# One head's K and V loaded in two pieces with different source shapes, in a two-layer decode kernel

## The chip, the cores and the metric

The kernel runs on one core of a Trainium2 chip. Its engines work side by side and meet at semaphores: PE (TensorE: matmuls, and PEld for its weight loads), DVE (VectorE), ACT (ScalarE), POOL (GpSimd) and SP (SyncE, which here only issues transfers). Transfers between the chip's main memory and the on-chip memory of 128 partitions are carried by 16 DMA engines. The metric is device microseconds of one launch, the median of several runs. Most runs of one kernel agree within a few tenths of a per cent. Beside the runs stands one profiled execution, whose trace gives the times of single instructions and packets.

## The reference

Two layers A and two layers B, in the order A, B, A, B, for a single token. A is attention of 32 heads over the last 4096 of 32768 cached keys, and B a mixer with a small MLP. With one token, the shifted part of the mixer is zero (every shifted slice falls off the end), so `w1` and `w2` don't count.

```python
def _A_ref(x, k_cache, v_cache, wq, wo):
    B, Sq, D = x.shape                     # 1, 1, 640
    Hq, Dh = 32, 192
    Hkv, Sk = k_cache.shape[1], k_cache.shape[2]
    W = min(4096, max(256, Sk // 4))       # 4096
    ...
    scores = jnp.einsum("bhqd,bhkd->bhqk", q, k) * (Dh ** -0.5)
    p = _softmax(scores, axis=-1)
    o = jnp.einsum("bhqk,bhkd->bhqd", p, v)
    return (lambda x, *d: x.transpose(*d))(o, 0, 2, 1, 3).reshape(B, Sq, Hq * Dh) @ wo

def _B_ref(x, w1, w2, w3, w4):
    ...
    h2 = _gelu(_layernorm(x1, axis=-1) @ w3) @ w4
    return x1 + h2

x = A_x
x = x + _A_ref(_layernorm(x, axis=-1), A_k_cache, A_v_cache, A_wq, A_wo)
x = x + _B_ref(_layernorm(x, axis=-1), B_w1, B_w2, B_w3, B_w4)
x = x + _A_ref(_layernorm(x, axis=-1), A_k_cache, A_v_cache, A_wq, A_wo)
x = x + _B_ref(_layernorm(x, axis=-1), B_w1, B_w2, B_w3, B_w4)
return x
```

Both layers A read the same K and V: 32 heads x 4096 keys x 192 bf16 values, twice.

## The kernel before

**Data.** The K of one head is 4096 rows of 384 bytes, contiguous in main memory. `Kw(h)` (L67) views it as 128 rows of 6144 values: partition p holds the 32 keys 32p to 32p + 31, 12,288 contiguous bytes. `Vw(h)` (L68) does the same for V. Each is loaded whole into one of 15 slots of that shape, by one DMA on SP's queue (`load`, L98 to L103). The same slots hold the five pieces of `wq` (L92 to L96), the transposed K, and the mixer's weights `w3` and `w4` with a half slot `half` (`load_w34`, L119 to L133). `wo` has its own two buffers (L107 to L112).

**Heads and groups.** The 32 heads form 8 groups of G = 4. Head h = 4g + i. For each head of the next group, `trans` (L254) transposes K on DVE in 32 x 32 blocks, in two halves (L258), and `kmm` (L268) multiplies it with the queries on PE (L280). For the current group `pv` (L337) multiplies the probabilities with V on PE (L349, L355, L360), `evac` scales by the softmax sum on DVE (L372 to L376), and `outproj` multiplies with `wo` (L383). `soft_a`, `soft_b`, `soft_c` (L291 to L333) make the softmax of a group: maximum over all keys of a head, exponentials on ACT (L314), sum over partitions by a matmul with ones (L322), and the probabilities brought into the layout of V. The order of the keys inside K and V matters only in that both have the same one.

**Order.** All of it is a fixed program order, written by hand: `attention` (L390) runs over the groups in `order` and, within a group, over the four heads, doing K work of the next group and V work of this one in turns. `plan` (L493) lists the loads in the order of their use: for each head the K of the next group, then the V of this one; after the second head `wo`; at the end of the layer the mixer's weights. Layer 1 takes the groups 0 to 7, layer 2 takes 7 to 0 and reuses the K (transposed), V and `wo` of what is still there: group 7's K and V are not loaded again, which leaves 60 K and 60 V loads in all.

**Queue.** All loads go through SP's queue in this order. A load waits on SP for its slot to be free (for the transpose or the matmul that read it last), and for the load issued eight before it: the loads use eight semaphores in turn. A load has landed when its semaphore has been increased by 16. Until then SP holds back only what is behind a waiting issue.

**The boundary.** The mixer (L459) reads `w3` (L470) and then `w4` (L487); its slots are free after that, and the K loads of layer 2 go into them. The last weights to come are the two loads of `half` (L129 and L130), which hold the last 20 of the 60 matmuls of L487 (w4's last chunks).

**PE's instructions.** The program is unrolled: 17,337 instructions on PE. They are fetched from main memory during the run, by DMA.

Of the kernel before, what the change touches and what calls it, by code (L numbers as in the profile page):

```python
# [16 lines left out]
P = 128  # L17
G = 4
ACT_TABLE_SET = 6
GELU_C = 0.044715  # L20
GELU_A = -2.0 * (2.0 / 3.141592653589793) ** 0.5
NSLOTS = 15


@with_exitstack
def kernel(
# [14 lines left out]
    nc = tc.nc  # L41
# [14 lines left out]
    NG = H // G  # L56
# [10 lines left out]
    Kw = lambda h: A_k_cache[0, h, s0:Sk, :].rearrange("(p j) d -> p (j d)", p=P)  # L67
    Vw = lambda h: A_v_cache[0, h, s0:Sk, :].rearrange("(p j) d -> p (j d)", p=P)  # L68
# [16 lines left out]

    free = deque(slots.tile([P, FREE], BF16, name=f"slot{n}", tag=f"slot{n}") for n in range(NSLOTS))
    half = slots.tile([P, HALF], BF16, name="half", tag="half")

    def slot():
        return free.popleft()  # L90

    wq_t = []  # L92
    for kc in range(ND):
        t = slot()
# [3 lines left out]
    def load(kind, h):  # L98
        if (kind, h) in resident:
            return  # L100
        t = slot()
        nc.sync.dma_start(t[:], (Kw if kind == "K" else Vw)(h))
        resident[(kind, h)] = t  # L103

    wo_t = {}

# [283 lines left out]
    def attention(order, xT_cur, xT_new, keep, loads):  # L390
        n_loaded = [0]

        def need(upto):
            while n_loaded[0] < min(upto, len(loads)):
                what = loads[n_loaded[0]]
                n_loaded[0] += 1
                if what[0] == "wo":
                    load_wo(what[1])
                elif what[0] == "w34":
                    load_w34()  # L400
                else:
                    load(*what)
# [155 lines left out]
```

## Time and profile before

| | us |
|---|---|
| median of 3 runs | 544.62 |
| lowest, highest | 543.62, 544.75 |
| the profiled execution, its own time | 543.57 |
| its span, first to last instruction | 541.3 |

| engine | busy us | share of the span |
|---|---|---|
| PE | 294.1 | 54% |
| PEld | 273.4 | 51% |
| DVE | 248.8 | 46% |
| ACT | 32.4 | 6% |
| POOL | 2.1 | 0% |

The page says further: 33,871 DMA packets, 219.42 MB, mean 405 GB/s; the granted clock of PE was 1.00 throughout. Times are microseconds from the start of the span. In lines of groups of instructions stand the line of the kernel, the engine, the operation, what it writes and reads, the count, and the mean duration. In the chain of waits each line has the start, the duration, and what ran: it follows the work that ended last back to what released it. SPq is SP's issuing of transfers. Two digit rows show the span in 40 equal slices, each digit the busy share in tenths. The tables by stretch give, for each stretch, its length, the busy time of each engine (with the count of instructions), the clock, the DMA share and the GB/s. A load from L102 took, in the median, 24.1 us (K) and 22.4 us (V) from issue to landing.

### The profile page before, as it was taken

To read this page: it belongs to the slowest core of one execution; us is meant where nothing else is said; L and a number is where in the kernel's file an instruction comes from. 1 tells how busy PE (TensorE), PEld (TensorE's weight loads), DVE (VectorE), ACT (ScalarE), POOL (GpSimd) and SP (SyncE) were. 2 spreads that over 40 slices of the span, in tenths; PEclk is the share of its full clock that TensorE was granted. 3 is DMA by queue.
4 is the path that set the end of the run, shared out by engine and by line. 5 is a ranking of instruction groups with operands and counts; after the bars stand their busy time and mean duration, and the time that the engine had idled before them with its cause. 6 is when DMAs were issued, how large, how long until landed. Compare 5 with 4: busy or idle time off the path is not lost.

```text
span 541.3 us, 18457 instructions
## 1 busy us (share of the span) xinstructions
PE 294.1 (54%) x8730; PEld 273.4 (51%) x8730; DVE 248.8 (46%) x360; ACT 32.4 (6%) x193; POOL 2.1 (0%) x11
## 2 busy tenths in 40 slices
PE   0144555663645536545475666655565655565654
PEld 0043554553645535544464656555555655555554
DVE  1185555354453555443502354565555455545402
ACT  1001010000101001010011100001010101010001
POOL 1000000000000000000000000000000000000000
DMA  8999999999999999999998899999999999999994
GB/s 347 429 426 412 423 422 411 425 411 423 417 418 425 409 424 414 421 422 412 417 410 305 354 420 427 422 413 421 410 423 421 411 421 412 420 420 416 417 401 160
DMA packets 33871, 219.42 MB, mean 405 GB/s; under 512 B 2692, under 2 KB 16516, under 8 KB 17796
## 3 DMA queue, kind: packets, MB, share of 16 engines
q1 hardware_dynamic: 33786, 218.25, 97.9%
q8 instruction: 68, 1.11, 0.8%
q14 instruction: 7, 0.06, 0.0%
q10 hardware_dynamic: 10, 0.00, 0.0%
HBM read 218.24 MB, written 0.00 MB: 403 GB/s over the span
## 4 chain that ended last, share of the span: by engine, by line
DMA 57%; DVE 18%; PE 16%; SPq 3%; issue 2%; ACT 2%; DVEq 0%
DMA slot<-in_A_k_cache_dram 36%; DVE slot L258 16%; DMA slot<-in_A_v_cache_dram 14%; DMA wo_g<-in_A_wo_dram 5%; PE S_ps L280 4%; PE O_ps L349 4%; PE O_ps L360 3%; SPq L129 2%; DMA half<-in_B_w_dram 2%; ACT E L314 2%; PE qT_ps L238 1%; PE l_ps L322 1%; PE nb_ps L308 1%; PE O_ps L355 1%; SPq L128 1%
## 5 line engine op out<-in xcount | busy, mean ns | idle before, releaser
L258 DVE STREAM_TRANSPOSE slot<-slot 128x1536 uint32<-128x1536 uint32 x120 | 206.0, 1756 | 94.7 <-PE O_ps L360 48.1
L280 PE MATMUL S_ps<-Qblk,slot 128*128 128x4 bf16 x3072 | 101.3, 167 | 180.1 <-DVE slot L258 179.6
L280 PEld LDWEIGHTS <-slot 128*128 128x128 bf16 x3072 | 91.3, 104 | 191.4 <-DVE slot L258 190.9
L349 PE MATMUL O_ps<-PT,slot 128*128 128x1 bf16 x2048 | 64.2, 165 | 8.2 <-DMA slot<-in_A_v_cache_dram 7.5
L349 PEld LDWEIGHTS <-slot 128*128 128x128 bf16 x2048 | 61.4, 104 | 13.5 <-DMA slot<-in_A_v_cache_dram 7.9
L360 PE MATMUL O_ps<-PT,slot 128*128 128x1 bf16 x1984 | 63.5, 166 | 2.0 <-issue 2.0
L360 PEld LDWEIGHTS <-slot 128*128 128x128 bf16 x1984 | 58.1, 105 | 3.1 <-issue 2.1
L372 DVE TENSOR_TENSOR osb<-O_ps,rl 128x2 bf16<-128x2 f32 x32 | 5.2, 162 | 72.1 <-PE O_ps L360 72.1
L310 ACT COPY nb_sb<-nb_ps 128x4 f32<-128x4 f32 x16 | 2.6, 162 | 444.3 <-PE nb_ps L308 444.3
L238 PE MATMUL qT_ps<-xn_bf,slot 128*128 128x1 bf16 x480 | 15.9, 165 | 18.3 <-DMA slot<-in_A_wq_dram 17.1
L238 PEld LDWEIGHTS <-slot 128*128 128x128 bf16 x480 | 14.5, 104 | 18.9 <-DMA slot<-in_A_wq_dram 17.5
L242 DVE TENSOR_TENSOR Xq<-qT_ps,maskq 128x24 bf16<-128x24 f32 x16 | 2.9, 182 | 41.1 <-PE qT_ps L238 41.1
L324 DVE RECIPROCAL rl<-l_ps 128x4 f32<-128x4 f32 x16 | 2.9, 179 | 33.2 <-PE l_ps L322 33.2
L314 ACT ACTIVATE E<-S_ps,nb_sb 128x32 bf16<-128x32 f32 x64 | 17.5, 286 | 0.5
L383 PE MATMUL y_ps<-osb,wo_g 128*128 128x1 bf16 x480 | 16.0, 166 | 1.0 <-DVE osb L372 1.0
L383 PEld LDWEIGHTS <-wo_g 128*128 128x128 bf16 x480 | 14.8, 104 | 1.5 <-issue 1.2
L322 PE MATMUL l_ps<-lpart,ones 128*128 128x4 f32 x32 | 9.4, 365 | 11.1 <-ACT E L314 11.1
L322 PEld LDWEIGHTS l_ps<-lpart,ones 128*128 128x128 f32 x32 | 8.0, 310 | 12.4 <-ACT E L314 12.4
L355 PE MATMUL O_ps<-PT,slot 128*64 128x1 bf16 x64 | 13.4, 210 | 0.0
L294 DVE TENSOR_REDUCE pm<-S_ps 128x4 f32<-128x128 f32 x16 | 4.7, 292 | 18.8 <-PE S_ps L280 18.8
L314 ACT ACTIVATION_READ_ACCUMULATOR E<-S_ps,nb_sb 128x1 f32 x64 | 13.0, 204 | 0.0
L308 PE MATMUL nb_ps<-dg,ones 4*128 4x4 f32 x32 | 9.3, 358 | 0.7 <-DVE dg L300 0.7
(80 smaller groups left out, 101.7 us busy)
## 6 DMA issues: line engine op xcount, KB each, us to landing
slot<-in_A_k_cache_dram SPq DMA_DIRECT2D x60, 1536.0 KB, 24.1
slot<-in_A_v_cache_dram SPq DMA_DIRECT2D x60, 1536.0 KB, 22.4
wo_g<-in_A_wo_dram SPq DMA_DIRECT2D x14, 960.0 KB, 28.2
slot<-in_A_wq_dram SPq DMA_DIRECT2D x5, 1536.0 KB, 13.0
slot<-in_B_w_dram SPq DMA_DIRECT2D x2, 1536.0 KB, 23.8
slot<-in_B_w_dram SPq DMA_DIRECT2D x2, 1120.0 KB, 19.6
half<-in_B_w_dram SPq DMA_DIRECT2D x2, 640.0 KB, 9.0
slot<-in_B_w_dram SPq DMA_DIRECT2D x2, 384.0 KB, 18.6
```

The lines of the kernel that those rows point to most:

```text
L128: nc.sync.dma_start(b[:, FB4:FREE], B_w4[NB4 * P:(NB4 + 1) * P, 0:FREE - FB4])
L129: nc.sync.dma_start(half[:, 0:D - P], B_w4[NB4 * P:(NB4 + 1) * P, P:D])
L238: nc.tensor.matmul(qT_ps[:, tl:tl + 1], lhsT=wq_t[kc][:, t * P:(t + 1) * P], rhs=xn_bf[:, kc:kc + 1], start=(kc == 0), stop=(kc == ND - 1))
L258: nc.vector.transpose(T[:, hf * HALF:(hf + 1) * HALF].bitcast(U32).rearrange("p (f j k) -> p j f k", f=NFB, j=HJ, k=32), Kn[:, hf * HALF:( ...
L280: nc.tensor.matmul(S_ps[:, i, hf * (NJQ // 2) + jq, :], lhsT=Tv[:, f, jq * P:(jq + 1) * P, t], rhs=Qblk[:, h * NCOL + 2 * f + t, :], start ...
L308: nc.tensor.matmul(nb_ps[:], lhsT=ones[0:G, :], rhs=sx[g]["dg"][0:G, :], start=True, stop=True)
L314: nc.scalar.activation(out=E[:, i], in_=S_ps[:, i], func=ACTF.Exp, bias=nb_sb[:, i:i + 1], scale=scale, accum_out=lpart[:, i:i + 1])
L322: nc.tensor.matmul(l_ps[:], lhsT=ones[:], rhs=d["lpart"][:], start=True, stop=True)
L349: nc.tensor.matmul(O_ps[:, pr, ca:ca + 1], lhsT=V[:, j * Dh + oa:j * Dh + oa + P], rhs=col(j), start=(j == 0), stop=(j == J - 1))
L355: nc.tensor.matmul(O_ps[r0:r0 + TB, pr, cc:cc + 1], lhsT=V[:, je * Dh + oc:je * Dh + oc + TB], rhs=col(je), start=True, stop=False, tile_p ...
L360: nc.tensor.matmul(O_ps[:, pr, cc:cc + 1], lhsT=V[:, j * Dh + oc - r0:j * Dh + oc - r0 + P], rhs=col(j), start=False, stop=(j == js[-1]), ...
L383: nc.tensor.matmul(y_ps[:, n:n + 1], lhsT=wo_t[g][:, 3 * pr + t, n * P:(n + 1) * P], rhs=osb[:, pr, t:t + 1], start=(first and t == 0 and ...
```

## The change

Four loads, those of K and V of head 13 (the second head of group 3, `(NG // 2 - 1) * G + 1`) in each layer, are issued as two DMAs. The first covers partitions 0 to 79 as before. The second covers partitions 80 to 127, 48 rows, with a source whose rows are regrouped: row b * 8 + a of the 48 goes to partition 80 + 6a + b, so that the source's outermost dimension is 8 and the next 6. K and V of this head are permuted in the same way. Nothing else is changed.

```diff
+R8 = 80
...
         t = slot()
-        nc.sync.dma_start(t[:], (Kw if kind == "K" else Vw)(h))
+        src = (Kw if kind == "K" else Vw)(h)
+        if h in split:
+            nc.sync.dma_start(t[0:R8, :], src[0:R8, :])
+            nc.sync.dma_start(t[R8:P, :], src[R8:P, :].rearrange("(b a) n -> a b n", a=8))
+        else:
+            nc.sync.dma_start(t[:], src)
         resident[(kind, h)] = t
+
+    split = {(NG // 2 - 1) * G + 1}
```

## The prediction

> **What bounds the kernel now.** I read the head of the page first, then the DMA part, then the chain of waits in order of time at the two places where a layer ends, and last the DMA increments inside the trace.
>
> ```profile
> span 541.3 us, 18457 instructions
> ...
> DMA  8999999999999999999998899999999999999994
> ...
> q1 hardware_dynamic: 33786, 218.25, 97.9%
> q8 instruction: 68, 1.11, 0.8%
> ...
> DMA 57%; DVE 18%; PE 16%; SPq 3%; issue 2%; ACT 2%; DVEq 0%
> ```
>
> No compute engine is busy for more than 54% of the span, while the sixteen DMA engines are busy in every slice; 57% of the chain is DMA. The kernel streams 218 MB, so its time is the time of the DMA engines. The small line is q8: 68 packets of instructions, 16,384 bytes each, run on the same engines as the data.
>
> The chain at the two ends of layers:
>
> ```profile
> 287.52 9.03 DMA half<-in_B_w_dram
> ...
> 296.60 0.71 PE y2T_ps L487 x20
> ...
> 504.58 22.66 DMA slot<-in_A_v_cache_dram
> ...
> 527.28 1.01 PE O_ps L349 x32
> ...
> 536.43 1.83 PE y2T_ps L487 x60
> ```
>
> Layer 1 ends on the landing of the last mixer weights (296.55); layer 2 on the landing of the last V (527.24), with 14.1 us of compute behind it. From 309 to 444 the chain runs through DVE and PE, but its groups of four heads take 29.4 us (338.57 to 367.94, both DVE L258), less than the stream needs for a group of nine loads (from #110 to #119 of the numbering below, 32.2 us between the first increments, 33.4 between the last), so compute is catching up there and the stream stays busy.
>
> A load counts as landed when all sixteen engines have added to its semaphore, and the trace holds the time of each increment. Sorted within a load, in us of the span (my numbering is SP's order of issue):
>
> ```
> load        first   8th     9th     last
> # 8 K       32.3    32.5    32.7    33.1
> #31 V      115.1   116.1   117.1   118.8
> #62 K      225.2   226.4   230.1   231.8
> #77 V      278.6   280.7   285.0   285.9
> #80 w4     286.5   288.5   292.8   294.4
> #84 K      299.0   299.3   299.3   300.5
> #110 K     395.2   396.6   396.9   399.0
> #145 V     520.3   522.0   526.0   527.2
> #150 half  529.9   530.3   534.5   535.8
> ```
>
> Eight engines fall behind the other eight: 0.8 us between first and last at the start, 7.3 at the end of layer 1, then a reset at the layer boundary (#84), and 7.0 again at the end. The lag comes in steps. After a q8 packet, one engine, and only one, adds 1.53 to 1.57 us later from then on; the next packet hits another, and after eight packets the same eight come round in the same order. 68 / 8 x 1.55 = 13.2 us per engine over the run, about 6.2 us in each layer, as the table shows. So half of the engines carry the instruction fetch of PE, and these eight set every landing; the other eight run dry at the boundary:
>
> ```profile
> 280.00:285.00 5.00, 2.76 (x81) 2.49 (x78) 0.38 (x3) 0.00 (x0) 0.00 (x0) 1.00 1.01 398
> 285.00:290.00 5.00, 3.05 (x81) 2.86 (x82) 0.71 (x6) 0.49 (x4) 0.00 (x0) 1.00 0.83 289
> 290.00:295.00 5.00, 1.99 (x62) 1.84 (x61) 1.98 (x10) 1.21 (x6) 0.00 (x0) 1.00 0.79 261
> ```
>
> The last two columns are the DMA share and GB/s: from 398 they drop to 261 while the slow half finishes.
>
> **The change, part by part.** Head 13's K and V, four of 120 such loads (#30 and #40 in layer 1, #107 and #117 in layer 2), become two issues each. Everything else on PE, DVE, ACT and POOL is the same in number and order; SP has four DMAs more. Bytes and packet size stay (12,288 bytes a row). The keys of rows 80 to 127 are permuted alike in K and V, and softmax with its sum doesn't care.
>
> *First piece, 80 rows:* spread like the 128-row loads, 5 rows on each engine instead of 8. *Second piece, 48 rows, source [8, 6, 6144]:* if the number of engines follows the outermost dimension, as the 5-row load of x shows (five 256-byte packets and five increments, where a 128-row load leaves sixteen), it runs on 8 engines with 6 rows each. Those eight then carry 11 rows per load, the other eight 5, against 8 before. One row is 0.461 us: increments of successive K/V loads on one engine are 3.69 us apart, divided by 8 (the median packet is 0.462). So per layer, two loads x 3 rows x 0.461 = 2.77 us move from one half of the engines to the other: a swing of 5.5 us against a lag of 6.2.
>
> *Which half?* This decides the sign. The x load marks five engines of that kind of choice. Packets of one engine follow each other without a gap (the next starts 3 to 4 ns before the end of the last), so chains can be followed: two of the five x engines go straight into their first wq row, and neither is hit by a q8 packet as far as I could follow it. The other three are among six engines that started within 60 ns of each other; three of these six are hit and three are not. Read as one pattern, the hit engines, in the order of the hits, start their first row early, early, late, late, early, late, late, late; the x engines' packets start at three early and two late times. If the halves are built alike and x takes the first five of the other half, that is early, early, late, late, early too. So I take it that the narrow piece goes to the eight engines without fetches.
>
> [...]
>
> *Layer 1.* Last V (#77): the fetch half lands at 285.9 - 2.77 = 283.1, the other half's last engine at 280.7 + 2.77 = 283.4; gain 285.9 - 283.4 = 2.5. Compute behind it moves by 2.5, so the first 40 of the matmuls L487 would end at 296.3 - 2.5 = 293.8. The last `half` load lands at 296.55 - 2.77 = 293.8 on the fetch half; the others, no longer idle, reach it at about 293.6. L487's last 20 start at some 293.95 instead of 296.60: gain 2.65. Layer 2's first loads wait for slots that the mixer and its first kmm free, so all of layer 2 moves by that.
>
> *Layer 2.* Last V (#145): fetch half 527.2 - 2.77 = 524.4, other half 522.0 + 2.77 = 524.8; gain 2.45. The mixer weights behind (#150, #151) gain 2.7 and don't hold it. Compute behind the V is unchanged.
>
> *Small costs.* Each extra DMA adds a 4-byte packet of 9 ns to its engines, some 15 ns with its neighbours, 0.06 us for four. SP's extra issue is 0.38 us (L102 median), hidden: loads are issued 22 to 24 us before they land. If it were on the path it would be 4 x 0.4 = 1.6 us. The second piece adds a wait for the increment of the load eight issues earlier, as its neighbours have; the loads behind it wait one issue longer, so that around the split 7 loads, 26 us, are under way instead of 8. The stream starves only when that falls to nothing. After V13 the other half is for a time about 2.3 us late (3.2 ahead before, less 5.5), but at #41 its last engine would add at 150.8 + 2.8 = 153.6, where the fetch half's last did at 153.9 before: no landing gets later.
>
> *Sum.* 2.65 + 2.45 - 0.06 = 5.0 us. The profiled execution took 543.57 (span 541.3 and 2.2 around it), so 538.5 for it. The median of the runs, 544.62, lies 1.05 above it; 539.6 against that. Ends: 5.5 us saved at most, 1.6 less if the issues were exposed.
>
> **The rivals.**
> 1. *Slower: the narrow piece falls on engines that fetch, all or some.* For: three of the five x engines are known only by a pattern. Against: two surely don't fetch. One fetching engine among the eight is enough, since the last increment counts: it takes 2.77 us more per layer, 5.5 in all: 550.1.
> 2. *Only one layer's share arrives.* For: from 309 to 444 the chain is compute, and K13 and V13 of layer 2 lie inside it; if slots rather than bytes pace the loads there, 2.45 is lost. Against: the increments of #87 to #145 come without a gap. 544.62 - 2.6 = 542.0.
> 3. *It doesn't do what it says:* the 48 rows spread over all sixteen engines, 3 each, 5 + 3 = 8 as before. For: no load in the trace has such a source. Against: x's five increments. 544.62 + 0.06 = 544.7.
>
> **How the numbers follow.** Forecast 0.78, rival 1 0.12, rival 2 0.06, rival 3 0.04. Runs of this kernel spread over 1.1 us around the median, and 0.2% is 1.1 us, about what can be told from no change. Time 539.6. The range runs from 538.0 (5.5 saved and 1 of spread) to 542.6 (rival 2 and the exposed issues taken in). Faster by over 0.2%: 0.78 + 0.06 = 0.84; within: 0.04; slower: 0.12.
>
> **What would show it.** Right: split loads with 8 data engines in the second piece; first-to-last spread of #77 and #145 about 3 us or less instead of 7; the DMA dip at the boundary nearly gone for 285 to 295; layer 1's last `half` landing near 294, the last V near 522.2. Wrong: a spread of 12 us at a layer's end (rival 1), layer 1 earlier but the last V earlier by no more than layer 1's gain (rival 2), the same lag steps and table as before (rival 3).

## The result and the profile after

| | us |
|---|---|
| after, median of 4 runs (lowest, highest) | 583.67 (582.36, 585.07) |
| before, 4 runs beside them | 544.68 (543.62, 545.11) |
| ratio, 95% interval | 1.072 (1.069 to 1.075) |
| the profiled execution after, its span | 583.91, 582.0 |

The change costs 39.0 us; the forecast was a gain of 5. The head of the page after, its row of GB/s, the DMA queues and the chain's shares:

```profile
span 582.0 us, 18465 instructions
...
DMA  8999999999999999999998999999999999999992
GB/s 358 427 423 413 422 412 424 293 327 425 282 282 421 414 421 414 423 421 411 417 386 290 368 424 425 411 422 307 304 421 296 248 422 414 418 421 413 415 366 78
DMA packets 33903, 219.42 MB, mean 377 GB/s; under 512 B 2724, under 2 KB 16548, under 8 KB 17828
...
q1 hardware_dynamic: 33818, 218.25, 97.3%
q8 instruction: 68, 1.11, 0.8%
...
DMA 55%; DVE 19%; PE 17%; SPq 3%; ACT 3%; issue 3%; DVEq 0%
```

Bytes, instruction fetches and the DMA busy digits are as before; there are 32 packets more, four times the eight 4-byte increments of a narrow piece (the second piece, on eight engines). What is new is in the GB/s row. Before it reads:

```profile
GB/s 347 429 426 412 423 422 411 425 411 423 417 418 425 409 424 414 421 422 412 417 410 305 354 420 427 422 413 421 410 423 421 411 421 412 420 420 416 417 401 160
```

Before, the only drop is at the layer boundary (305, 354). After, there are four more, at slices 7 and 8, 10 and 11, 27 and 28, 30 and 31 (counted from 0): one for each load that the change cuts. Against some 420 GB/s they come to about 35 us, most of the 40.7 by which the span grew. The same by stretch, the last column being GB/s and the one before it the DMA share; first four stretches of the changed kernel, of which the second and fourth hold K and V of head 13 (K13 and V13 below):

```profile
core 0: us, PE busy (x) PEld busy (x) DVE busy (x) ACT busy (x) POOL busy (x), PEclk, DMA share, GB/s
90.00:106.00 16.00, 7.50 (x229) 6.74 (x226) 8.04 (x10) 0.00 (x0) 0.00 (x0) 1.00 1.01 424
109.00:121.00 12.00, 3.68 (x112) 3.40 (x112) 3.41 (x2) 0.27 (x1) 0.00 (x0) 1.00 1.00 193
125.00:145.00 20.00, 9.46 (x303) 8.92 (x303) 9.44 (x11) 0.00 (x0) 0.00 (x0) 1.00 1.02 424
150.00:169.00 19.00, 6.69 (x209) 6.04 (x209) 7.50 (x7) 0.27 (x1) 0.00 (x0) 1.00 1.04 215
```

and the middle two of the kernel before:

```profile
109.00:121.00 12.00, 6.78 (x223) 6.45 (x223) 7.23 (x6) 0.23 (x1) 0.00 (x0) 1.00 1.02 411
125.00:145.00 20.00, 10.35 (x299) 9.62 (x299) 10.81 (x13) 1.61 (x10) 0.00 (x0) 1.00 1.01 424
```

The DMA share stays at 1.00 while the bytes fall to half: the engines are occupied, not productive. Each packet of 12,288 bytes takes longer: 1021 ns in the mean (900 in the median) over those that start between 109 and 121, where 462 is usual, and 96% of them take over 800. The trace doesn't name the engine of a packet, but with so few fast ones all sixteen must be slow. PE and DVE do about half as much in 109 to 121 because they wait for K. In the list of waits of the changed kernel that is the line

```profile
DVE slot L266 <- DMA slot<-in_A_k_cache_dram: 90.0, 25, 10.9
```

(us in total, times, longest); before, the same wait was 45.7 us in 16 times, 4.8 at most.

The increments of each load, numbered and sorted as in the prediction (one cut load adds one issue, so the numbers move by up to four):

```
load after / before   first            last             spread after / before
#34  / #33           127.9 / 121.5    133.3 / 125.2     5.5 / 3.7
#79  / #77  (last V) 293.3 / 278.6    304.1 / 285.9    10.8 / 7.3
#86  / #84           316.9 / 299.0    319.2 / 300.5     2.2 / 1.6
#149 / #145 (last V) 555.9 / 520.3    566.7 / 527.2    10.8 / 7.0
```

Two things have happened. The leading engines, too, are some 15 us late at the end of layer 1, and the lag between engines has grown by 3.5 us instead of shrinking. The experiments take them apart.

### The profile page after: what moved, and what is told of

Its sections match the earlier page's. It is cut to its first block, busy times and chain, and to the rows that moved or that the text cites. A ratio compares the mean times of both kernels' runs of the same rounds, so it can differ in the third digit from the quotient of the medians.

```text
span 582.0 us, 18465 instructions
## 1 busy us (share of the span) xinstructions
PE 295.5 (51%) x8730; PEld 274.0 (47%) x8730; DVE 248.9 (43%) x360; ACT 32.4 (6%) x193; POOL 2.1 (0%) x11
## 3 DMA queue, kind: packets, MB, share of 16 engines
q8 instruction: 68, 1.11, 0.8%
## 4 chain that ended last, share of the span: by engine, by line
DMA 55%; DVE 19%; PE 17%; SPq 3%; ACT 3%; issue 3%; DVEq 0%
DMA slot<-in_A_k_cache_dram 43%; DVE slot L266 17%; DMA slot<-in_A_v_cache_dram 9%; PE S_ps L288 4%; PE O_ps L357 4%; PE O_ps L368 3%; ACT E L322 2%; SPq L136 2%; DMA half<-in_B_w_dram 2%; PE l_ps L330 1%; DMA slot<-in_A_wq_dram 1%; SPq L108 1%; PE nb_ps L316 1%; PE pmT_ps L304 1%; PE qT_ps L246 1%
## 5 line engine op out<-in xcount | busy, mean ns | idle before, releaser
L246 PEld LDWEIGHTS <-slot 128*128 128x128 bf16 x480 | 14.5, 104 | 18.6 <-DMA slot<-in_A_wq_dram 17.3
L250 DVE TENSOR_TENSOR Xq<-qT_ps,maskq 128x24 bf16<-128x24 f32 x16 | 2.9, 182 | 40.7 <-PE qT_ps L246 40.7
L330 PEld LDWEIGHTS l_ps<-lpart,ones 128*128 128x128 f32 x32 | 8.0, 313 | 11.8 <-ACT E L322 11.8
```

Of the source, the lines that this page charges most:

```text
L246: nc.tensor.matmul(qT_ps[:, tl:tl + 1], lhsT=wq_t[kc][:, t * P:(t + 1) * P], rhs=xn_bf[:, kc:kc + 1], start=(kc == 0), stop=(kc == ND - 1))
L330: nc.tensor.matmul(l_ps[:], lhsT=ones[:], rhs=d["lpart"][:], start=True, stop=True)
```

## The experiments

Each ran once with a profile, beside a run of the kernel before on the same chip: 543.33 (first four), 543.34 (next four), 543.92 (two) and 543.49 us (the last). "A load" below (as in "6.8 us a load") means the loss divided by the number of loads touched. The diffs are against the change, or against the kernel before where that is said. One of them, the sixteen-engine variant, asks which share of the loss each of the two things has; the others ask what the larger one is.

**Cut by columns.**

```diff
-            nc.sync.dma_start(t[0:R8, :], src[0:R8, :])
-            nc.sync.dma_start(t[R8:P, :], src[R8:P, :].rearrange("(b a) n -> a b n", a=8))
+            nc.sync.dma_start(t[:, 0:HALF], src[:, 0:HALF])
+            nc.sync.dma_start(t[:, HALF:FREE], src[:, HALF:FREE])
```

> Four theories for the 39 us (9.8 us for each of the four split loads). S, shared ways into SBUF: a row's partition decides which way into SBUF it takes, a load of all 128 partitions loads all ways evenly, and a piece of fewer partitions does not. R, regrouped source: the rows that are read in eight groups are slow. C, the cut: a second DMA in a load costs by itself. N, narrow: the eight engines that carry the second piece have six rows instead of three and hold everybody up. Here the load is cut by columns, both pieces on all 128 partitions and plain. S: 544.7, within 2 us. R: 544.7. N: 544.7. C: 570 to 584.

Measured 544.45, 1.1 above the run beside it, within the spread of the kernel before (543.33 to 545.11 here); the GB/s row has no drop but the boundary's:

```profile
GB/s 349 422 432 405 429 421 414 420 412 421 414 419 426 408 428 410 423 421 412 419 405 308 354 418 426 425 410 423 407 422 420 412 425 407 425 417 416 418 395 141
```

The second issue, its semaphore and its wait are not the cost. C falls.

**The same cut, second piece plain.**

```diff
-            nc.sync.dma_start(t[R8:P, :], src[R8:P, :].rearrange("(b a) n -> a b n", a=8))
+            nc.sync.dma_start(t[R8:P, :], src[R8:P, :])
```

> Same cut at partition 80, but the second piece is loaded plainly, 3 rows on each of 16 engines. S: slower still, 557 to 572 (in the first piece five rows of an engine took 3.82 us in the trace, the time of eight, so 1.5 us too much; in the second three rows an engine into 48 partitions lose about as much or more; 3 to 7 us for each of four loads). R: 544.7. N: 544.7. C: 584.

Measured 570.56: 27.2 us, 6.8 a load. So 27 of the 39 us come from cutting by partitions alone, with neither a regrouped source nor a narrow piece. The stretches at K and V of head 13, behind an undisturbed one:

```profile
90.00:106.00 16.00, 7.61 (x239) 7.07 (x237) 8.05 (x10) 0.00 (x0) 0.00 (x0) 1.00 1.01 425
109.00:118.00 9.00, 3.68 (x112) 3.40 (x112) 3.44 (x2) 0.27 (x1) 0.00 (x0) 1.00 1.01 231
150.00:161.00 11.00, 4.75 (x158) 4.47 (x156) 4.59 (x3) 0.00 (x0) 0.00 (x0) 1.00 1.02 213
```

425 against 213: half. R and N can't be the main cause.

**Cut in the middle.**

```diff
-            nc.sync.dma_start(t[0:R8, :], src[0:R8, :])
-            nc.sync.dma_start(t[R8:P, :], src[R8:P, :].rearrange("(b a) n -> a b n", a=8))
+            nc.sync.dma_start(t[0:64, :], src[0:64, :])
+            nc.sync.dma_start(t[64:P, :], src[64:P, :])
```

> Two plain pieces of 64 partitions, each 4 rows on each of 16 engines. S: if 64 neighbouring partitions have half of the ways, four rows of an engine take the time of eight, 3.7 us instead of 1.85, in both pieces: 3.7 us for each of four loads, 559.5 (552 to 563). R: 544.7. N: 544.7. C: 584.

Measured 571.0: 27.7 us, 6.9 a load. S has the sign, and its size is too small by 3.2 us a load: a cut load's own rows at half speed are 3.7, and something costs as much again. The trace says where. From when the leading engines enter the first piece until the last engines leave the second, nearly all rows take around 900 ns, also those of the whole load before, which the late engines still carry, and of the whole load behind, which the leading engines have begun. Rows of over 700 ns start and end within 13.8 us at K13 and 17.0 at V13 in layer 1, where 7.4 would do for eight rows at half speed. The last run of this section tests that.

**Narrow piece in front.**

```diff
-            nc.sync.dma_start(t[0:R8, :], src[0:R8, :])
-            nc.sync.dma_start(t[R8:P, :], src[R8:P, :].rearrange("(b a) n -> a b n", a=8))
+            nc.sync.dma_start(t[P - R8:P, :], src[P - R8:P, :])
+            nc.sync.dma_start(t[0:P - R8, :], src[0:P - R8, :].rearrange("(b a) n -> a b n", a=8))
```

> The regrouped piece, six rows on each of eight engines, goes to partitions 0 to 47, and the plain piece to 48 to 127. The same number of DMAs, rows and engines as in the change; only the partitions are other ones. S: the eight engines of the narrow piece no longer write into the half that the other eight are writing into with their next loads, so most of the loss of the second piece goes: 546 to 560. R, N and C: 584, as the change.

Measured 577.17: 33.8 us, 5.2 less than the change lost. A miss for S as I had priced it: I had put the loss on the second piece, but a plain piece of 80 rows seems to cost wherever it lies. It is a miss for the others too, since only the partitions, and the rows of the source that belong to them, differ from the change.

**One DMA, another assignment.**

```diff
-            nc.sync.dma_start(t[0:R8, :], src[0:R8, :])
-            nc.sync.dma_start(t[R8:P, :], src[R8:P, :].rearrange("(b a) n -> a b n", a=8))
+            nc.sync.dma_start(t[:], src.rearrange("(b a) n -> a b n", a=16))
```

> What the first four runs leave: a plain cut at partition 80 or 64 costs 26 us (some 7 us a load), and from the first row of the first piece to the last of the second nearly all rows of all 16 engines take 850 to 950 ns, twice the usual 462. Two theories. P, paths: each engine's usual rows have a path into SBUF that no other engine uses, and a piece gives rows to engines whose usual rows lie elsewhere, so that two engines share one path. H, halving: any DMA that covers fewer than 128 partitions halves the traffic of all engines for as long as an engine is in it, whatever the partitions. Here nothing is cut: one DMA of all 128 partitions, its source regrouped to an outermost dimension of 16, so that it has eight rows for each of 16 engines as before, but each engine's rows go to eight neighbouring partitions. P, if that is not the usual assignment: slow rows as in a cut, 560 to 575. H: 544.7. If the regrouped reading itself is slow (R, of the first four runs): 560 to 575 too.

Measured 568.39: 25.1 us, 6.3 a load.

```profile
90.00:106.00 16.00, 7.53 (x237) 6.99 (x235) 8.05 (x10) 0.00 (x0) 0.00 (x0) 1.00 1.01 422
109.00:118.00 9.00, 3.67 (x113) 3.39 (x112) 3.44 (x2) 0.27 (x1) 0.00 (x0) 1.00 1.02 217
150.00:162.00 12.00, 5.88 (x190) 5.54 (x191) 5.03 (x4) 0.00 (x0) 0.00 (x0) 1.00 1.02 216
```

Nothing is cut here. There is no piece; one DMA writes all 128 partitions, and the traffic halves all the same, 217 and 216 GB/s after 422. H falls, and what is left of the theories is P, that it counts which engine writes which partitions. That is by elimination: eight rows on each engine, to eight neighbouring partitions, is my estimate from the load of x (five rows, five increments), and no trace names the engine of a row. Regrouped reading as such is excluded by the next run.

**Sixteen in place of eight.**

```diff
-            nc.sync.dma_start(t[R8:P, :], src[R8:P, :].rearrange("(b a) n -> a b n", a=8))
+            nc.sync.dma_start(t[R8:P, :], src[R8:P, :].rearrange("(b a) n -> a b n", a=16))
```

> The change with 16 in place of 8: the second piece is regrouped but spread over 16 engines, three rows each. It tells what of the 13 us between the change (584) and the plain cut (570.6) is regrouping and what is the eight engines. R (regrouped reading is slow): 580 to 584. N (six rows on each of eight engines, which are the late ones): 570.6, within 2 us, with the first and the last increment 7.4 to 7.9 us apart at the end of the layers as in the plain cut, where the change had 10.8 to 12.

Measured 570.12, the time of the plain cut (570.56): reading regrouped rows costs nothing that can be told, and the lag at the last V of both layers is 7.4 us, not the 10.8 of the change. What the eight engines add is 39.0 - 27.2 = 11.8 us (each against the run of before beside it). The forecast's row price would make it 12 rows x 0.461 = 5.5 us on the engine that ends last; at half speed, in which these rows run, it is 11.1. That is worked out, not measured by itself. "Narrow piece in front" fits: at partitions 0 to 47 the narrow piece adds 33.8 - 27.2 = 6.6, near the full-speed price, if a plain piece of 80 rows costs the same at 48 to 127 as at 0 to 79.

**Added rows at partitions 0 to 63** (against the kernel before).

```diff
-        nc.sync.dma_start(t[:], (Kw if kind == "K" else Vw)(h))
+        src = (Kw if kind == "K" else Vw)(h)
+        nc.sync.dma_start(t[:], src)
+        if h in extra:
+            for r in (0, 32):
+                nc.sync.dma_start(half[r:r + 32, :], src[r:r + 32, 0:HALF].rearrange("(b a) n -> a b n", a=8))
```

> The four loads are whole and plain as before; behind each, two more DMAs write 32 rows of 6,144 B into partitions 0 to 31 and 32 to 63 of a tile that nothing reads then, each with a source regrouped to eight (four rows on each of eight engines). Added work, so the time alone measures the cost of such a piece. Eight rows at half of 0.462 are 1.85 us for each of the eight engines. P, if these partitions are those engines' own: no slow rows; 4 times 1.85 = 7.4 us more if the eight engines are the late ones, 551 to 553, and 544.7 if they are the others. H: everything at half speed while an engine is in it, at least the spread of 2.3 to 5 us between engines and 1.85 to 3.7 us of rows at each load, so 560 to 572.

Measured 550.28: 6.9 us, against 7.4 expected. No slow stretch at any of the four places; the added rows of 6,144 bytes take 235 ns in the median, half of the 462 of a whole row:

```profile
90.00:106.00 16.00, 7.66 (x241) 7.12 (x239) 8.05 (x10) 0.00 (x0) 0.00 (x0) 1.00 1.01 424
109.00:121.00 12.00, 6.69 (x224) 6.32 (x219) 7.33 (x7) 0.27 (x1) 0.00 (x0) 1.00 1.01 407
150.00:169.00 19.00, 7.99 (x255) 7.54 (x255) 7.25 (x9) 0.00 (x0) 0.00 (x0) 1.00 1.01 414
```

Eight engines write 32 partitions at a time here (the page has 64 packets under 512 bytes more than before, 2,756 against 2,692: eight increments for each of the eight pieces), with a regrouped source, in the middle of a full stream, and nobody slows: 407 and 414 GB/s. This run also shows which engines the narrow pieces take, because without slow rows the increments can be read. A load in the middle of layer 1, sorted:

```
before, #62:  225.2 225.4 225.5 225.6 225.9 226.1 226.2 226.3 | 230.1 230.5 230.6 230.7 230.8 230.9 231.0 231.8
here,   #66:  225.8 226.2 | 229.2 229.2 229.4 229.8 229.8 230.2 | 230.4 230.6 230.8 230.9 231.0 231.0 | 233.6 235.3
```

The increments don't name their engines, so this is read from the sorted times: two early engines stay within 1 us of where they were, six early ones are 3 to 4 us later (two loads of 1.85), six late ones stay, and two late ones are 3 to 4 us later still. So the eight engines of a narrow piece are six without instruction fetches and two with. My expectation spoke of "the late ones" as if it were all or none: two are enough, since a load has landed with its last increment. The changed kernel has the same pattern at #79: 293.3 and 293.6, then twelve from 297.8 to 300.2, then two at 304.1.

**Added rows at partitions 64 to 127** (the same diff with `for r in (64, 96)`).

> The same two added DMAs at partitions 64 to 95 and 96 to 127. P, if those are the other eight engines' own: the eight rows take twice as long, 3.7 us at each load, and rows of the other eight engines do too, 555 to 565 (4 times 3.7 is 14.8, so 559.5), 3 to 8 us more than at partitions 0 to 63. If the result is the other way round, the eight engines' own partitions are the upper ones. H: the same time as at partitions 0 to 63, within 2 us.

Measured 564.81: 21.5 us, 14.5 more than the same rows at partitions 0 to 63, and slow rows at each of the four places (the added ones take 464 ns in the median):

```profile
112.00:120.00 8.00, 3.52 (x112) 3.33 (x112) 3.55 (x3) 0.00 (x0) 0.00 (x0) 1.00 1.00 238
153.00:161.00 8.00, 5.39 (x175) 5.07 (x174) 3.88 (x4) 0.00 (x0) 0.00 (x0) 1.00 1.05 231
```

The number of engines, rows and bytes and the form of the source are the same; the destination differs, and with it the rows read (`src[64:96]` in place of `src[0:32]`, and so on). At K13 the two runs moved 407 and 238 GB/s. This pair is the cleanest evidence for P, which reads it as eight engines with a way of their own to partitions 0 to 63 and a shared one to 64 to 127; the ways themselves no run shows. In all of these runs but the one DMA regrouped to 16, the half of the block that is read moves with the half that is written, so the place of reading is a rival that no run was made for. The trace of the kernel before speaks against it: in the load of `w3` (L121) each partition takes four rows of 3,072 bytes from the four quarters of a block of the same 1536 KB, and its first and last increments follow those of the last V by 3.8 us (278.6 to 282.4, 285.9 to 289.7), where K and V loads are 3.7 apart. The time is inside P's range for it, but the distance between the two places is 14.5 where I had 3 to 8: the half speed seems to last longer than the shared rows do.

**One plain piece, 64 rows** (against the kernel before; partitions 0 to 63, then 64 to 127).

```diff
+        if h in extra:
+            nc.sync.dma_start(half[0:64, :], src[0:64, 0:HALF])
```

> The four loads whole as before; behind each one more DMA, plain, 64 rows of 6,144 B into partitions 0 to 63 of a tile that nothing reads then: four rows on each of 16 engines, 4 x 0.231 = 0.92 us of work for each. It asks how long the half speed lasts when only one kind of half is written. Simple pairing (an engine is slow only while it and another really write through one path, and the late eight own partitions 0 to 63): the rows take twice as long, 1.85 us a load, 552 in all, and the late eight in the piece are as slow as the early eight. Lasting (half speed for everybody from the first engine's entry to the last one's exit, so the lag of 2.3 to 3.5 us comes on top): 4.2 to 5.4 us a load, 561 to 566.

> The same at partitions 64 to 127. Simple pairing: the late eight's rows meet the early eight's next loads, 552. Lasting: 561 to 566, as at partitions 0 to 63. If the two places differ by over 3 us, then it matters which group of engines is in the piece while the other is in its own loads.

Measured 560.19 and 562.17, 4.1 and 4.6 us a load for 0.92 us of rows (the estimate of the expectation, four rows of 0.231). The stretch at K13, at the lower and then at the upper partitions:

```profile
112.00:118.00 6.00, 2.71 (x88) 2.60 (x88) 0.28 (x1) 0.00 (x0) 0.00 (x0) 1.00 1.03 227
112.00:118.00 6.00, 2.71 (x88) 2.60 (x88) 0.82 (x2) 0.00 (x0) 0.00 (x0) 1.00 1.02 241
```

Simple pairing (552) falls at both; "lasting" holds at the upper partitions and is missed by 0.8 us at the lower ones. (The premise in the text that the late eight own partitions 0 to 63 doesn't fit: by the sorted increments above, of the eight engines whose rows ran at full speed there two are late.)

**Cut where the lag is small and where it is large** (the middle cut, other heads).

```diff
-    split = {(NG // 2 - 1) * G + 1}
+    split = {1, (NG - 2) * G + 1}
```

> Two plain pieces of 64 partitions again, but for another two heads in each layer, one that is loaded early in the layer (head 1), where the eight late engines are some 1 us behind the others, and one late (head 25), where they are 5 to 6 us behind: eight cut loads in the program instead of four. P with the time that it lasts: traffic is at half speed from when the first engine enters a cut load to when the last one leaves it, so a load costs its own 3.7 us and once more the lag between the two groups of engines (the four cuts in the middle lost the leading engines 6.1, 7.2, 6.2 and 7.3 us at a spread of 3.2 to 5.4). So here an early one 4 to 5.5 us, a late one 8 to 10 us, and in all 544.7 + 4 x 4.7 + 4 x 9 = 599 (590 to 608). A fixed cost for each cut: 6.7 us each, early and late alike, 598 in all: the time doesn't tell the two apart, the shifts of the increments at the two places do.

Measured 599.65, 56.2 us for eight loads. As said there the sum doesn't decide, the places do. By the shift of the last increment against the kernel before, each cut load cost, in order of time: 4.5, 5.4, 8.3, 8.6 us in layer 1 and 2.5, 6.3, 11.7, 9.2 in layer 2 (which runs through the groups backwards, so head 25 is its early one), 56.5 in all. The spread between first and last increment just ahead of the cuts was 0.6, 1.9, 5.8 and 6.6 us in layer 1 and 2.4, 2.3, 6.8 and 9.6 in layer 2. Early and late differ as expected, though the 2.5 (the cut right behind the layer boundary) lies below the range given and the 6.3 and 11.7 above theirs. Slow stretches of layer 1:

```profile
10.00:24.00 14.00, 1.59 (x30) 1.19 (x30) 0.44 (x2) 0.00 (x0) 0.00 (x0) 1.00 1.01 430
26.00:32.00 6.00, 2.58 (x79) 2.26 (x79) 3.88 (x4) 0.00 (x0) 0.00 (x0) 1.00 0.99 209
52.00:58.00 6.00, 3.52 (x112) 3.33 (x112) 3.59 (x3) 0.00 (x0) 0.00 (x0) 1.00 1.00 190
214.00:230.00 16.00, 7.30 (x201) 6.67 (x198) 4.01 (x6) 1.61 (x10) 0.00 (x0) 1.00 1.01 214
259.00:275.00 16.00, 5.60 (x178) 5.10 (x177) 7.06 (x5) 0.27 (x1) 0.00 (x0) 1.00 1.02 218
```

Speed is about half in all four; what differs is for how long: 9 to 10 us early, 18 to 19 late. A fixed cost per cut falls. My estimate from these shifts: the price of a cut load in this stream is its own 3.7 us once more, plus very roughly the lag between the engines: that sum is within 2 us for six of the eight, but 6.1 for the load that cost 2.5 and 13.3 for one that cost 9.2.

**What stays open.** Why the traffic stays at half when the leading engines are already in the piece at partitions 64 to 127 while the late ones are in that at 0 to 63, two places that don't share a way if P is right about the pair of added rows. The packets show only that most rows take 900 ns or so; the assignment of a plain piece of 48, 64 or 80 rows to the sixteen engines is not visible in the trace. No version was found that beats the kernel before: relieving the fetching engines needs rows that other engines can write at full speed, and of the forms tried that confine rows to some engines only the narrow piece at partitions 0 to 63 ran so (407 and 414 GB/s), on two of the fetching engines.

## Why the prediction was wrong

- *The stream bounds the kernel; eight engines carry PE's fetches and lag.* Right. A delay of the stream reached the end almost in full (in the profiled executions 39.5 us at the last V and 40.7 in the span), and 7.4 us of rows added to eight engines, two of them late, gave 6.9. (That the fetches, 68 packets and 1.11 MB on q8, are PE's is an estimate: 17,460 of the 18,457 instructions before are PE's. These are its matmuls and weight loads on the page; the 17,337 in the part on the kernel before is not borne out. Nothing rests on it.)
- *"It runs on 8 engines with 6 rows each."* Right on the engines: eight data increments in each of the four pieces, so rival 3 falls. The six rows are 48 divided by 8.
- *"So I take it that the narrow piece goes to the eight engines without fetches."* Wrong by two of the eight. The reading rested on a pattern in the starts of five packets, two of which were sure; the rest was filled in by symmetry. Rival 1 had the rule: "One fetching engine among the eight is enough". Its 550.1 would be the time by the prediction's own sum if rows had kept their price; the lag at the end of layer 1 grew from 7.3 to 10.8 us, 3.5 where that rival has 2.77. The chance of 0.12 was too low for a reading with three unknown engines in it.
- *"Spread like the 128-row loads, 5 rows on each engine instead of 8", at 0.461 us a row.* This is the step that decided. The sixteen engines are right (the 32 packets more leave sixteen increments to each first piece); that each has five of the rows no run shows. The 0.461 came from whole loads of 128 rows, and it was carried to pieces of 80 and 48. No row of the trace before showed such a piece, so the price should have been bounded, with twice the price (0.92) as its upper end; the rows of the stretches at K13 and V13 took 0.90 and 0.88 us in the median. At 0.92 for the eight rows of a cut load, four loads cost 4 x 3.7 = 14.8 us, and the range would have reached to 559.4. The rest of the 27.2 us that the plain cut cost goes with the lag, during which nearly everything stays at half speed (why, is open); the other 11.8 of the 39.0 come with the narrow piece, 5.5 of them at the forecast's price.
- *Small costs.* Right: with two issues for each of the four loads and full width, the time was 1.1 us longer, within the spread.
- *"No landing gets later"* after V13: wrong, by 18 us at the end of layer 1.

## What to carry to other kernels

The price read from full-width transfers, 0.46 us a row, did not hold for pieces cut by partitions, where rows took about 0.9. Before cutting a load by partitions, or regrouping its outermost dimension, time the rows of one such load; cutting by columns left the stream whole here (544.45 against 570.56 for a cut by partitions). Read the GB/s row beside the DMA busy row: in these runs a stream at half speed had the same busy digits (9 at 282 GB/s as at 425).

## What the runs showed of the hardware

- A load cut by partitions, or whole and regrouped to an outermost dimension of 16, ran at half (190 to 231 GB/s where 422 to 430 are usual), with nearly all rows slow for 13.8 us at K13 and 17.0 at V13 of the middle cut. That other engines than usual write the partitions is P's reading. The cost of the same cut went from 2.5 to 11.7 us, small where the engines were 0.6 to 2.4 us apart and large where they were 5.8 to 9.6.
- Eight narrow pieces of 32 rows, with outermost dimension 8, cost 6.9 us in all at partitions 0 to 63 (407 GB/s at K13), and 21.5 at partitions 64 to 127 (238).
- The eight engines that fetch instructions are not the eight that a narrow piece takes: of those, two fetch and six don't, as the sorted increments show (six early ones and two late ones 3 to 4 us later).
